# Loading the last query chunks of two batches late, on a kernel of linear attention followed by a two-layer ELU network

## The chip, the cores and the metric

The kernel runs on one core of one Trainium2 chip. The metric is the device time of one execution in microseconds, and lower is better. A change counts as faster or slower when it passes 2%. The span, from the first to the last traced instruction, is about 2 us shorter than the time.

## The reference, cut to what matters

```python
def _attn_ref(q, k, v):                      # q, k, v: 8 batches, 8 heads, 576 rows, 64 wide
    q_s = exp(q - max(q, -1));  q_s /= sum(q_s, -1)      # over the head's width
    k_s = exp(k - max(k, 2));   k_s /= sum(k_s, 2)       # over the sequence
    kv = einsum('bhsd,bhse->bhde', k_s, v)               # needs ALL of k and v of a batch
    return einsum('bhsd,bhde->bhse', q_s, kv)            # each row of q alone
def _moe_ref(x, w_in, w_out):                # x: 4608 x 512, w_in: 512 x 2048
    h = x @ w_in
    g = where(h > 0, h, exp(min(h, 0)) - 1)              # ELU
    return g @ w_out                                     # 4608 x 512
```

The asymmetry that the change uses is in the comments. A batch's kv needs every row of k and v. An output row needs only its own row of q.

## The kernel before

The program works in 9 blocks of 512 rows of x, but a batch has 576 rows, which are 9 chunks of 64. So block 0 takes chunks 0 to 7 of batch 0, and its ninth chunk is left for block 1. Of batch 1, block 1 takes 7 chunks and leaves 2. `split(b)` says where the cut is, and `ao_rest` makes the product for the leftover chunks. A *unit* is half a batch (4 heads), so q0 and q1 belong to batch 0, q2 and q3 to batch 1. `hg` is a group of hidden columns (256 of 2048) of one block, `kv` the k-v product, `W1` is w_in and `W2` w_out. A list scheduler orders the instructions of each engine from estimated durations; TensorE keeps its program order.

```python
    @staticmethod
    def split(b):
        if b < 2:
            return 8 - b
        ...

    def q_part(self, n, key):          # exp on ScalarE, sum and reciprocal on VectorE; all 9 chunks
        ...
    def q_mul(self, n, key, dmat):     # QS = exp(q) / sum, all 9 chunks
        ...
        S.add("dve", 1400, lambda e: e.tensor_tensor(qso, raw[:, :, :, :], rz, ALU.mult), ...)

    def tp(self, n, ps, key, evac="act"):      # transpose QS on TensorE, units 0 to 3 only
        ...
        def mm(e):
            for c in range(CH):                # CH = 9
                o = c * 128 if c < 5 else 1024 + (c - 5) * 128
                last = e.transpose(t16[:, o:o + 128], self.QS[al][:, c, :], self.ID[:, :])
            return last
        ...                                    # two evictions, of 5 and 4 chunks

    def exp_k(self, n, key):
        ek, flat = self.ek(n % 2), self.raw_flat(n % 2, "k")
        self.S.add("act", t_act(1152, False), lambda e: e.activation(...AF.Exp), ...)

    def program(self):
        ...
        for n, h in ((0, 0), (0, 1), (1, 0), (1, 1)):      # q of batch 0: unit 0 on SP, unit 1 on GpSimd
            src = self.src["q"][0, 4 * h + 2 * n:4 * h + 2 * n + 2, :, :].rearrange(
                "f (p c) d -> (f p) (c d)", c=CH)          # rows of 2304 bytes
            ...
        for n, t in ((0, "k"), (0, "v"), (1, "k"), (1, "v")):
            gp = self.load(n, t, "gp", -80, follow=gp)     # everything from here on: GpSimd's queue
        for s in range(4):
            gp = self.load_w1(s, -60, follow=gp)           # 4 parts of W1, 4 loads each
        ...
        self.hg_mm(0, 0, 3, (1,))
        self.hg_mm(0, 1, 2, (1,))
        self.ao_rest(0, 1, -60)                            # leftover of batch 0: in the startup
        for what in (0, "2q", 1, "3q", 2, "2k", "2v", "3k", "3v", 3, 4, 5):   # numbers: parts of W2
            ...
        for j in range(NBLK):
            for g in range(8):
                self.hg(j, g, order[g % 4], key, "gp" if j or g > 2 else "act" if g == 1 else "dve", ...)
            ...
            if j == 0:
                work = dict(zip((6, 9, 11, 19), (
                    lambda: self.tp(2, C, key), lambda: self.tp(3, Dd, key), lambda: kv([2, 3]),
                    first)))
            ...
            if j == 0:
                elem_q(2, k1)
                self.ao_rest(1, Dd, key)                   # leftover of batch 1: end of block 0
```

The softmax here doesn't subtract the row's maximum and nothing guards it: scores larger than these inputs give would overflow.

Of the kernel before, what the change touches and what calls it, by code (L numbers as in the profile page):

```python
# [18 lines left out]
CH = 9  # L19
# [16 lines left out]
class Sched:  # L36
# [49 lines left out]
    @staticmethod  # L86
    def parts(names):

        return [y for x in names for y in ([x + "h0", x + "h1"] if x in ("vR0", "vR1") else [x])]
# [168 lines left out]
class Gen:  # L258
# [13 lines left out]
    def alloc(self):  # L272
# [21 lines left out]
        self.RZK = [self.RZ[:, i, :] for i in range(2)]  # L294
        self.SEEN = a("SEEN", [16, 4, 16], F32)
# [35 lines left out]
    def load_half(self, n, t, h, key, follow):  # L331
# [6 lines left out]
                          tag=f"ld {t}{n}")  # L338

# [43 lines left out]
    def q_part(self, n, key):  # L383
# [3 lines left out]
        halves = (0, 1) if n < 2 else (slice(0, 2),)  # L387
        for h in halves:
            part = raw[:, h]
            part = part.rearrange("p c d -> p (c d)" if n < 2 else "p h c d -> p (h c d)")  # L390
            S.add("act", t_act(1152 // len(halves), False),
                  lambda e, part=part: e.activation(part, part, AF.Exp), key,  # L392
                  X=[self.q_res(n)[h]] if n < 2 else self.q_res(n), low=True, tag=f"expq{n}")
        for h in halves:
            z, src = zq[:, h], raw[:, h]
            if n > 1:
                z, src = z.rearrange("p h c -> p (h c)"), src.rearrange("p h c d -> p (h c) d")
            S.add("dve", 1350 if n > 1 else 750, lambda e, z=z, src=src: e.tensor_reduce(  # L398
                z, src, AX.X, ALU.add), key, R=self.q_res(n) if n > 1 else [f"qR{n}h{h}"],
                W=[f"ZQ{i}h0", f"ZQ{i}h1"] if n > 1 else [f"ZQ{i}h{h}"], low=True, tag=f"red{n}")  # L400
        S.add("dve", 270, lambda e: e.reciprocal(self.RZQ[i][:, :, :], self.ZQ[i][:, :, :]),
# [3 lines left out]
    def q_mul(self, n, key, dmat):  # L405
# [4 lines left out]
        rz = self.RZQ[i][:, :, :].unsqueeze(3).broadcast_to([128, 2, CH, D])  # L410
        qso = self.QS[al][:, :, :].rearrange("p c (h d) -> p h c d", h=2)
        S.add("dve", 1400, lambda e: e.tensor_tensor(qso, raw[:, :, :, :], rz, ALU.mult),  # L412
              key, R=qR + [f"RZQ{i}"], W=[f"QS{al}"], low=True, tag=f"mul{n}", port=True)
        if dmat:
# [3 lines left out]
                R=[f"QS{al}"], W=qR, dma=f"tp{i}{dmat}", nbytes=128 * 2304 * (4 if n < 4 else 1), low=True, tag=f"dtp{n}")  # L418
# [35 lines left out]
    def tp(self, n, ps, key, evac="act"):  # L454

        S = self.S
# [3 lines left out]

        def mm(e):
            for c in range(CH):
                o = c * 128 if c < 5 else 1024 + (c - 5) * 128
                last = e.transpose(t16[:, o:o + 128], self.QS[al][:, c, :], self.ID[:, :])
            return last
        S.add("pe", CH * 56 + 110, mm, key, R=[f"QS{al}", "ID"], X=bk, tag=f"tp{n}")
        for x, (c0, c1, o) in enumerate(((0, 5, 0), (5, 9, 1024))):
# [3 lines left out]
            if evac == "act" or x == 0:  # L471
                S.add("act", t_act(w, True), lambda e, dst=dst, src=src: e.activation(
                    dst, src, AF.Copy), key, W=[f"qsT{al}{x}"], X=[bk[x]], tag=f"evq{n}")
            else:
# [37 lines left out]
    def exp_k(self, n, key):  # L512
        ek, flat = self.ek(n % 2), self.raw_flat(n % 2, "k")
        self.S.add("act", t_act(1152, False), lambda e: e.activation(
            ek[:, :, :, :], flat.rearrange("p (h c d) -> p h c d", h=2, c=CH), AF.Exp),
            key, X=[f"kR{n % 2}"], low=True, tag=f"expk{n}")
# [90 lines left out]
    def ao_rest(self, b, ps, key, x=1):  # L607
# [4 lines left out]
        at = b * CH + c0  # L612
        for n in (2 * b, 2 * b + 1):
            i = n % 2

            def mm(e, i=i):
                for f in range(2):
                    last = e.matmul(P[:, f * 512 + i * w:f * 512 + i * w + w], self.MBLK[i][:, f, :],  # L618
                                    self.qsT[i][:, c0:c1, f * 64:f * 64 + 64], start=True, stop=True)
# [141 lines left out]
    def program(self):  # L761
# [6 lines left out]
        for n, h in ((0, 0), (0, 1), (1, 0), (1, 1)):  # L768
            src = self.src["q"][0, 4 * h + 2 * n:4 * h + 2 * n + 2, :, :].rearrange(
                "f (p c) d -> (f p) (c d)", c=CH)  # L770
            dst = self.RQ[n][:, h, :, :].rearrange("p c d -> p (c d)")
            eng = "gp" if n else "sp"
            op = S.add(eng, 450 if eng == "sp" else 760, lambda e, src=src, dst=dst: e.dma_start(dst, src),  # L773
                       -90, W=[f"qR{n}h{h}"], dma=f"q{n}h{h}", nbytes=128 * 2304,
# [8 lines left out]
        for n, t in ((0, "k"), (0, "v"), (1, "k"), (1, "v")):  # L783
            gp = self.load(n, t, "gp", -80, follow=gp)
# [177 lines left out]
```

## Time and profile before

| | before |
|---|---|
| time, median of 3 runs | 297.72 us (297.61 to 297.74) |
| time and span of the profiled run | 298.25 us, 296.4 us |
| TensorE busy | 98% of the span |
| idle time of its weight loads after 13.66 us | 0.49 us ahead of hidden group 4, 1.15 us ahead of batch 1's kv |

The last row comes from the timeline of the weight-load engine of the kernel before. Its columns are start, duration, engine, line, operation, operands and count, with the idle time ahead and its releaser in brackets. These are the lines of the two holes and the one ahead of the first:

```profile
16.41 5.33 PEld L654 LDWEIGHTS PS<-XT,W 128*128 128x128 f32 x24
22.24 7.15 PEld L654 LDWEIGHTS PS<-XT,W 128*128 128x128 f32 x32 [0.49 <-DVE GT L676]
...
42.59 0.67 PEld L491 LDWEIGHTS PS<-VB,KR 64*64 64x64 bf16 x72 [1.15 <-DVE VB L442]
```

I call these two places gates: TensorE reaches hidden group 4 of block 0 and may wait for W1's third part, and it reaches batch 1's kv and may wait for v. After the second gate it never waits again.

### The profile page before, as it was taken

To read this page: it belongs to the slowest core of one execution; us is meant where nothing else is said; L and a number is where in the kernel's file an instruction comes from. 1 tells how busy PE (TensorE), PEld (TensorE's weight loads), DVE (VectorE), ACT (ScalarE), POOL (GpSimd) and SP (SyncE) were. 2 spreads that over 40 slices of the span, in tenths; PEclk is the share of its full clock that TensorE was granted. 3 is DMA by queue.
4 is the path that set the end of the run, shared out by engine and by line. 5 is a ranking of instruction groups with operands and counts; after the bars stand their busy time and mean duration, and the time that the engine had idled before them with its cause. 6 is when DMAs were issued, how large, how long until landed. Compare 5 with 4: busy or idle time off the path is not lost.

```text
span 296.4 us, 4373 instructions
## 1 busy us (share of the span) xinstructions
PE 290.6 (98%) x1840; PEld 235.8 (80%) x1840; DVE 149.6 (50%) x167; ACT 152.3 (51%) x177; POOL 123.1 (42%) x133
## 2 busy tenths in 40 slices
PE   7999999999999999999999999999999999999995
PEld 2578878887888888878888888888878888888885
DVE  6857951978346913692268416760661046105600
ACT  5666366963666375546554565537541455125411
POOL 8998200762187035713372237313740055005500
PEclk9999999999999999999999999999999999999999
DMA  7999988927992598039901990099002210131022
GB/s 238 320 391 390 390 286 291 394 95 132 311 229 112 182 356 162 0 94 347 260 3 30 375 287 10 2 328 213 1 0 58 46 42 0 45 75 25 0 65 77
DMA packets 36675, 49.37 MB, mean 167 GB/s; under 512 B 16688, under 2 KB 17456, under 8 KB 36656
## 3 DMA queue, kind: packets, MB, share of 16 engines
q1 hardware_dynamic: 29872, 34.29, 40.5%
q0 software_dynamic: 6320, 14.29, 15.8%
q10 hardware_dynamic: 464, 0.53, 0.5%
q8 instruction: 14, 0.23, 0.3%
q14 instruction: 5, 0.04, 0.0%
HBM read 36.70 MB, written 9.44 MB: 156 GB/s over the span
## 4 chain that ended last, share of the span: by engine, by line
PE 85%; DMA 7%; POOL 6%; issue 0%; DVE 0%; ACT 0%; POOLq 0%
PE PS L700 41%; PE PS L654 39%; DMA VR<-in_v_dram 7%; POOL W L347 3%; PE PS L491 2%; PE PS L584 2%; PE PS L618 1%; POOL W L358 1%; POOL KR L315 1%; POOL VR L315 0%; POOL QR L315 0%; POOL QR L773 0%; DVE VB L442 0%; ACT OSB L733 0%; POOL ID L749 0%
## 5 line engine op out<-in xcount | busy, mean ns | idle before, releaser
L683 DVE SCALAR_TENSOR_TENSOR GT<-ESB,PS 128x1024 fp32r<-128x1024 f32 x69 | 84.0, 1221 | 116.6 <-POOL ESB L680 116.5
L700 PE MATMUL PS<-W,GT 128*128 128x512 f32 (+1 forms) x592 | 136.4, 386 | 0.0
L654 PE MATMUL PS<-XT,W 128*128 128x512 f32 x576 | 133.0, 390 | 0.1
L654 PEld LDWEIGHTS PS<-XT,W 128*128 128x128 f32 x576 | 107.8, 188 | 22.9 <-DVE GT L676 0.5
L700 PEld LDWEIGHTS PS<-W,GT 128*128 128x128 f32 x592 | 108.0, 188 | 21.6
L680 POOL TENSOR_SCALAR ESB<-ESB 128x1024 f32<-128x1024 f32 x69 | 73.7, 1075 | 100.1 <-ACT ESB L668 100.1
L668 ACT ACTIVATE ESB<-PS 128x1024 f32<-128x1024 f32 x72 | 73.8, 1028 | 51.5 <-PE PS L654 51.5
L714 ACT ACTIVATE OSB<-PS 128x512 f32<-128x512 f32 x35 | 20.7, 598 | 55.5 <-PE PS L700 55.1
L438 POOL CAST VB<-VR 128x1152 bf16<-128x1152 f32 x12 | 14.5, 1212 | 46.6 <-DMA VR<-in_v_dram 46.6
L398 DVE TENSOR_REDUCE ZQ<-QR 128x18 f32<-128x1152 f32 (+1 forms) x18 | 21.7, 1212 | 2.6 <-ACT QR L392 2.6
L412 DVE TENSOR_TENSOR QS<-QR,RZQ 128x1152 f16<-128x1152 f32 x16 | 21.5, 1353 | 0.4
L392 ACT ACTIVATE QR<-QR 128x1152 f32<-128x1152 f32 (+1 forms) x18 | 18.6, 1054 | 4.1 <-DMA QR<-in_q_dram 4.0
L425 POOL CAST qsT<-QR 128x1152 fp32r<-128x1152 f16 x12 | 13.8, 1152 | 10.0 <-DMA QR<-QS 10.0
L432 ACT ACTIVATE KR<-KR 128x1152 bf16<-128x1152 f32 x14 | 15.9, 1169 | 3.8 <-DMA KR<-in_k_dram 3.8
L604 ACT ACTIVATE XT<-PS 128x640 fp32r<-128x640 f32 (+1 forms) x12 | 8.2, 738 | 15.4 <-PE PS L584 15.4
L347 POOL DMA_DIRECT2D W<-in_moe_w_in_dram x16 | 10.0, 1357 | 0.0
L640 PE MATMUL PS<-IDLE 128*128 128x512 f32 (+1 forms) x14 | 8.5, 732 | 1.5 <-DVE IDLE L752 1.5
L358 POOL DMA_DIRECT2D W<-in_moe_w_out_dram x6 | 9.1, 2416 | 0.0
L628 ACT ACTIVATE XT<-PS 128x1024 fp32r<-128x1024 f32 (+3 forms) x8 | 6.8, 846 | 1.1 <-PE PS L618 1.1
L491 PEld LDWEIGHTS PS<-VB,KR 64*64 64x64 bf16 x504 | 4.7, 107 | 3.3 <-DVE GT L683 1.8
L584 PE MATMUL PS<-qsT,MBLK 128*128 128x320 f32 (+3 forms) x32 | 7.1, 338 | 0.0
L640 PEld LDWEIGHTS PS<-IDLE 128*128 128x128 f32 (+1 forms) x14 | 2.6, 210 | 5.6 <-issue 2.3
(46 smaller groups left out, 83.8 us busy)
## 6 DMA issues: line engine op xcount, KB each, us to landing
out_dram<-OSB SPq DMA_DIRECT2D x67, 128.0 KB, 3.6
QR<-in_q_dram SPq DMA_DIRECT2D x12, 576.0 KB, 8.6
KR<-in_k_dram SPq DMA_DIRECT2D x12, 576.0 KB, 6.1
VR<-in_v_dram SPq DMA_DIRECT2D x12, 576.0 KB, 6.8
W<-in_moe_w_in_dram POOLq DMA_DIRECT2D x16, 256.0 KB, 9.6
W<-in_moe_w_out_dram POOLq DMA_DIRECT2D x3, 1024.0 KB, 16.3
KR<-in_k_dram POOLq DMA_DIRECT2D x4, 576.0 KB, 13.6
VR<-in_v_dram POOLq DMA_DIRECT2D x4, 288.0 KB, 14.6
```

The lines of the kernel that those rows point to most:

```text
L347: "gp", 530, lambda e, kc=kc: e.dma_start(self.W1[:, kc, sl], w[kc, :, :, sl]), key,
L392: lambda e, part=part: e.activation(part, part, AF.Exp), key,
L398: S.add("dve", 1350 if n > 1 else 750, lambda e, z=z, src=src: e.tensor_reduce(z, src, AX.X, ALU.add), key, R=self.q_res(n) if n > 1 else ...
L412: S.add("dve", 1400, lambda e: e.tensor_tensor(qso, raw[:, :, :, :], rz, ALU.mult), key, R=qR + [f"RZQ{i}"], W=[f"QS{al}"], low=True, tag= ...
L432: S.add("act", t_act(1152, False), lambda e: e.activation(ek[:, :, :, :], flat.rearrange("p (h c d) -> p h c d", h=2, c=CH), AF.Exp), key, ...
L438: self.cv[n] = S.add("gp", 1250, lambda e: e.tensor_copy(VB[:, :, :, 0:D], raw[:, :, :, :]), key, R=rv, W=[f"VB{i}0", f"VB{i}1"], low=True ...
L654: last = e.matmul(P[:, t * 512:(t + 1) * 512], self.W1[:, kc, tt * 128:(tt + 1) * 128], self.XT[:, kc, rc:rc + BLK], start=(kc == 0), stop ...
L668: S.add("act", t_act(1024, True), lambda e: e.activation(esb[:, :], P[:, :], AF.Exp), key, W=[f"E{i}"], X=self.banks(ps), tag=f"exp{j}.{g}")
L680: S.add("gp", 1120, lambda e: e.tensor_scalar(esb[:, :], esb[:, :], 1.0, 0.0, ALU.min, ALU.max), key, X=[f"E{i}"], tag=f"min{j}.{g}", port ...
L683: S.add("dve", t_dve(1024), lambda e: e.scalar_tensor_tensor(gt, esb[:, :], -1.0, P[:, :], ALU.add, ALU.max), key, R=[f"E{i}"], W=gw, X=se ...
L700: last = e.matmul(dst, GT[:, jj, ts * 128:(ts + 1) * 128], self.W2[:, jj, cols], start=(jj == 0), stop=(jj == 15))
L714: S.add("act", t_act(512, True), lambda e: e.activation(osb[:, :], src, AF.Copy), key, W=[f"O{i}0", f"O{i}1"], X=[f"b{bk}"], tag=f"evo{jb} ...
```

## The change

The intent is to keep out of the load queue, in the first 42 us, what is not needed there. The ninth chunk of batch 0's q goes from in front of k to the middle of W1's first part, and chunks 7 and 8 of batch 1's q go behind W2. The two leftover products move to where a later block needs them. W2's loads stay as they are. The diff, cut to its core (helpers for resource names, evictions and hints to the scheduler are left out):

```diff
@@ q_part, q_mul: for units 0 and 1 only the first 8 chunks @@
+        w = self.split(0) if n < 2 else CH
@@ new @@
+    def load_q1(self, n, part, eng, key, after=(), follow=None):   # "m": 7 chunks, "r": 2 chunks
+        cs = slice(0, self.split(1)) if part == "m" else slice(self.split(1), CH)
+        ...
+    def q_piece(self, n, part, key):       # exp, sum, reciprocal, multiply of one part
+        ...
+        if part == "r":                    # and, for 2 chunks: transpose by DMA on SP, cast on GpSimd
+            ...
+    def load_last(self, key, follow):      # ninth chunk of both units: 512 rows of 256 bytes
+        src = self.src["q"][0, :, :, :].rearrange(
+            "(h u f) (p c) d -> c (f p) (h u) d", h=2, u=2, c=CH)[CH - 1]
+        ...
+    def q_last(self, key):                 # its exp, sum, reciprocal, two multiplies
+        ...
@@ tp @@
-            for c in range(CH):
+            for c in range(count):         # count = 8; chunk 7 of batch 0 holds the ninth chunk's rows
@@ exp_k: two halves for k1 @@
+        for h in (slice(0, 2),) if n == 0 else (slice(0, 1), slice(1, 2)):
@@ program @@
-                "f (p c) d -> (f p) (c d)", c=CH)
+                "f (p c) d -> (f p) (c d)", c=CH)[:, 0:w * D]          # rows of 2048 bytes
...
+            if (n, t) == (1, "k"):
+                for h in range(2):
+                    gp = self.load_half(n, t, h, -80, gp)
+                continue
...
-            gp = self.load_w1(s, -60, follow=gp)
+            gp = self.load_w1(s, -60, follow=gp, kcs=(0, 1))
+            if s == 0:
+                gp = self.load_last(-60, gp)
+            gp = self.load_w1(s, -60, follow=gp, kcs=(2, 3))
...
-        self.ao_rest(0, 1, -60)
+        self.q_last(-60)
...
+            elif what[1] == "q":
+                gp = self.load_q1(int(what[0]), "m", "gp", -50, follow=gp)
...
-                self.hg(j, g, order[g % 4], key, "gp" if j or g > 2 else "act" if g == 1 else "dve",
+                self.hg(j, g, order[g % 4], key, "gp" if j or g > 3 else "act" if g % 2 else "dve",
...
+                if j == 0:
+                    for n in (2, 3):
+                        self.ldq = self.load_q1(n, "r", "sp", key, after=self.w2, follow=self.ldq)
...
-                    work = dict(zip((6, 9, 11, 19), (
-                        lambda: self.tp(2, C, key), lambda: self.tp(3, Dd, key), lambda: kv([2, 3]),
-                        first)))
+                    def both():
+                        self.ao_rest(0, Dd, key)
+                        kv([2, 3])
+                    work = dict(zip((6, 8, 11, 19), (
+                        lambda: self.tp(2, C, key), lambda: self.tp(3, Dd, key), both, first)))
+                elif j == 1:
+                    def both():
+                        self.ao_rest(1, Dd, key)
+                        ...
+                        convert(2, key)
+                        ...
+                        kv([n0, n1])
+                    work = {5: both, 12: aos}
...
-                self.ao_rest(1, Dd, key)
```

## The prediction

> **What bounds the kernel now.** I read the page first: one core, span 296.4 us, granted clock full in every slice. Then the chain of waits, which tells where the end is set.
>
> ```profile
> PE 290.6 (98%) x1840; PEld 235.8 (80%) x1840; DVE 149.6 (50%) x167; ACT 152.3 (51%) x177; POOL 123.1 (42%) x133
> ...
> DMA  7999988927992598039901990099002210131022
> ```
>
> ```profile
> 5.80 9.89 POOL W L347 x16
> ...
> 20.37 0.45 POOL VR L315
> 20.82 21.23 DMA VR<-in_v_dram
> 42.05 0.02 issue
> 42.07 0.48 DVE VB L442
> 42.55 0.04 issue
> 42.59 0.77 PE PS L491 x68
> 43.37 2.06 PE PS L700 x8
> ...
> 48.46 14.59 PE PS L654 x64
> ```
>
> The columns of the second fence are start, duration, what. From 42.59 us to the end at 293.45 the chain is TensorE alone, one piece after the other without a gap: 250.9 us of pure matrix work. Before 42.59 it isn't TensorE but a queue of transfers: GpSimd issues them all by 22 us, and the last unit of v for batch 1 lands at 42.05. The DMA digits of the page are 8 or 9 through most of this stretch. So a change can gain in two ways only: let batch 1's kv product (L491) start before 42.59, or take matrix work out of what follows it.
>
> Next, how TensorE spends the time up to 42.59: the windows view, cut where TensorE's idle times are (columns: length of the window, busy time of each engine with counts, clock, DMA share, GB/s), and the waits of the first 50 us.
>
> ```profile
> 13.66:21.80 8.14, 8.14 (x40) 6.75 (x38) 4.26 (x6) 4.56 (x7) 8.14 (x15) 1.00 1.28 394
> 21.80:22.24 0.44, 0.37 (x2) 0.00 (x1) 0.14 (x1) 0.44 (x2) 0.44 (x5) 1.00 1.28 377
> 22.24:41.44 19.20, 19.17 (x97) 15.71 (x98) 14.42 (x15) 10.48 (x12) 7.92 (x10) 1.00 1.23 390
> 41.44:42.59 1.15, 0.42 (x2) 0.00 (x0) 0.79 (x2) 1.15 (x3) 0.00 (x0) 1.00 1.10 299
> ```
>
> ```profile
> PEld PS L491 <- DVE VB L442: 1.2, 1, 1.2
> ...
> PEld PS L654 <- DVE GT L676: 0.5, 1, 0.5
> ```
>
> Two holes in the weight loads. At 41.44 they stop for 1.15 us until v is converted. The same place one block later has an idle time of 0.35 us that is put down to issue, so about 0.80 us is a real wait. At about 21.8 they stop for 0.5 us, before hidden group 4 of block 0. The view blames VectorE, but the elu that frees group 4's bank (group 0's) ended at 20.66 in the timeline. Group 4 also needs the third part of W1, and the trace's landing record of the twelfth W1 load ends at 22.4; such records end some 0.2 us after their reader starts (k of unit 0: record 8.72, its exp starts at 8.51). So that hole is W1's, and the DMA stream paces TensorE at both. Where nothing waits, 64 matmuls take 14.51 us (227 ns each).
>
> In the startup the same stream gates: exp of k1 waits for k1 until 11.48, v1 lands at about 12.85 and its kv product starts at 13.02, the first W1 load lands at about 13.55 and the first hidden matmul starts at 13.66.
>
> **What the Trainium skill says.** "DMA: Bandwidth & Descriptors", section "Issuing engines are not separate DMA queues": loads from any engine share the same 16 DMA engines. The trace agrees: the stream moves 390 GB/s whatever is in it, so bytes taken out of GpSimd's queue and loaded later count as time only while that queue is the gate. The same page, "Specifications", puts the size for line rate at 512 B or more, and "Why small descriptors are slow (HBM only)" gives 11 cycles in place of 8 for 256 B. No load in this trace has such rows, so I take it as an estimate for the new 256 B rows. "Anatomy of one DMA — SWDGE (gpsimd) path" puts most of a fixed 2 us into the receipt of the last byte. Here the bytes nearly stop at 42.6 (35 GB/s from 43 to 44), while the last W2 landing is recorded at 44.85, so a landing can come 2 us after its bytes.
>
> **The change, part by part.**
>
> (a) Batch 0's q loads lose the ninth chunk: 4 x 32 KB = 128 KB less in front of k0. At 390 GB/s that is 0.33 us, which all of k0, v0, k1, v1 and the first two W1 loads should land earlier. k1 in two halves lets ACT's exp after the last landing be about 0.68 in place of 1.16 us. But v1 (12.85) and W1 (13.55) gate next, so only 0.33 us of it counts: first hidden matmul at about 13.3.
>
> (b) The ninth chunks come back as one load of 128 KB in 512 rows of 256 B, after two of W1's sixteen loads. At the full rate 0.33 us, with twice the cost for short rows 0.67 us; I take 0.33 to 0.65. So every later load of GpSimd's queue is 0 to 0.3 us later than before, until (d). GpSimd's own issue (two more, 0.7 to 1 us each) is hidden: the first W1 load is issued at 5.7 and lands at 13.6.
>
> (c) The leftover product of batch 0 (L618, four matmuls, 0.53 us of TensorE at 16.08) leaves the startup and goes just ahead of batch 1's kv. The hidden groups 0 to 3 then run 0.3 + 0.5 us sooner, and TensorE reaches group 4 at about 21.0 in place of 21.8. There it meets W1's twelfth load, which now lands at 22.2 to 22.5 in place of 22.2. The whole startup gain becomes a longer wait at group 4 (about 1.3 in place of 0.45 us).
>
> (d) q2 and q3 lose 2 of 9 chunks: 2 x 128 KB, 0.66 us less in front of v3. With (a) and (b), v3 lands 0.33 - (0.33 to 0.65) + 0.66, so 0.35 to 0.65 us earlier, at 41.4 to 41.7. The conversion takes 0.46 us and the hop 0.05, so v lets kv start at 41.9 to 42.25.
>
> (e) TensorE's arrival at kv: before, 22.24 + 19.55 = 41.79 (42.59 less the 0.80 of real wait). After: 22.2 to 22.5, plus 19.55, plus 0.55 for batch 0's leftover, less 0.11 for one transpose fewer in each of the two groups of nine (0.51 us for nine weight loads): 42.2 to 42.5. This is later than v's 41.9 to 42.25, so TensorE and no longer v sets the start: about 42.3, a gain of 0.3 us.
>
> (f) After kv: batch 1's leftover product (0.40 us at 48.06) moves from the end of block 0 into block 1, and costs the same there. Its two chunks, now a separate small piece for each unit, add per unit an exp of 256 (about 0.42 us on ACT), reduction, reciprocal and multiply (about 1.0 us on DVE), a small DMA transpose and a cast of 0.4 us on GpSimd. VectorE is idle for 5.56 us before 52.58, and the leftover is wanted only at about 69, so this is beside TensorE's work. The casts of q4 and q5 (2.25 us from 72.35, their data landing only then) are followed by their product at 75.42; moving their place in the program behind the leftover (about 69) takes nothing from that.
>
> (g) ELU of groups 2 and 3 by VectorE and ACT, not GpSimd: it keeps a GpSimd busy with issuing (until about 25) out of group 3's chain, whose bank is needed at 27.7 and was freed at about 27.3. Protection, no gain by itself.
>
> Sum: (e) -0.3 us, the rest 0: 297.72 - 0.3 = 297.4 us.
>
> **The rivals.**
>
> First rival: v stays the gate. If the short rows cost nothing, W1 lands on time and TensorE arrives at 42.2, v at 41.9; if TensorE also waits less at group 4, the start falls to the v gate and the gain is up to 0.65 us (297.1). One thing could bring that: a 16 KB instruction fetch at 18.25 takes 1.16 us on one DMA engine, and from there the spread between the first and last of the sixteen completions of a load grows from 1.05 to 2.3 us, which delays W1's third part and all later landings. The change removes 12 matrix instructions before that point, so it may come later in the W1 stream. I reckon some 0.7 us later, still before the twelfth W1 load.
>
> Second rival: the leftover of batch 0 waits for the eviction of the transposed q3, which in the kernel before ran from 41.62 to 42.79, behind exp of k3. If ACT's order stays so, the leftover starts near 42.4 and kv near 42.9: 0.3 us slower (298.0). Against it: the transposes of q3 come two plan steps nearer to those of q2 than before, and one eviction of 1024 replaces two, so ACT should do it before k3 lands at about 40.
>
> Third rival: the added pieces of (f) upset an in-order queue (SP's transposes, GpSimd's mins) in block 1 and leave a hole in TensorE's 14.5 us runs. There is room on every engine, so I give it a tenth, and 0.3 to 1 us.
>
> **Range and chances.** The gate times leave 0 to 0.6 us of gain; the two losses pull the other way by 0.3 to 0.5, and runs scatter by 0.1: 296.8 to 298.1. Two per cent would be 6 us. The whole of TensorE's waiting after 13.66 is 1.3 us, so faster by 2% is excluded by the sum, and slower by 2% would need a stall of a kind that I don't see.
>
> **What would show it.** In the changed profile: first hidden matmul at about 13.3; no L618 piece near 16; a hole of about 1 us in the weight loads before group 4, ending at 22.2 to 22.5; the kv product at about 42.3 right behind batch 0's leftover, with little or no wait on v's conversion; then an unbroken chain of TensorE of 250.8 us. Wrong would be: group 4 starting before 22, a wait on ACT's eviction ahead of the leftover, or new holes between 48 and 80.

## The result, and the profile after

| | time, median | range | runs | span, median |
|---|---|---|---|---|
| before, same chip | 297.73 us | 297.61 to 297.79 | 4 | |
| after | 298.05 us | 297.60 to 298.45 | 4 | 295.95 us |

The ratio is 1.0011, with a 95% interval of 0.9994 to 1.0028: the same. The prediction was 297.4 us, "same", 296.8 to 298.1. The range held, but the small gain that I expected is not there.

The profiled run of after was its fastest, 297.60 us. First the counts and the DMA digits from its page:

```profile
PE 289.2 (98%) x1836; PEld 235.8 (80%) x1836; DVE 151.3 (51%) x177; ACT 153.1 (52%) x180; POOL 123.3 (42%) x136
...
DMA  7999988978991696039902990098002110230022
...
q8 instruction: 14, 0.23, 0.3%
```

Four matmuls less, and ten more instructions on VectorE. The DMA digits are the same 8 or 9 up to 59 us; the one that moved most is the ninth (59 to 66 us), 7 in place of 2, where loads behind W2 now fall, and no gate lies there. The third line, the same in both pages, will matter later: 14 packets of 16 KB are instruction fetches, and they travel on the same DMA engines as the loads. The chain of waits of after:

```profile
16.39 12.97 PE PS L740 x56
29.37 6.35 PE PS L786 x28
...
38.54 2.81 PE PS L786 x12
41.35 0.37 PE PS L704 x4
41.72 0.74 PE PS L573 x67
42.45 2.05 PE PS L786 x8
...
47.17 14.51 PE PS L740 x64
```

The chain of before was a queue of transfers up to 42.05. Here it is TensorE from 16.39 on: hidden groups (L740) without a hole at group 4, out products (L786), then batch 0's leftover (L704, four matmuls) and kv (L573) right behind it. The weight-load timeline of after says the same; beside the lines of before, the hole at 22.24 is gone and kv starts at 41.67 in place of 42.59:

```profile
16.36 12.58 PEld L740 LDWEIGHTS PS<-XT,W 128*128 128x128 f32 x56 [0.61 <-DVE XT L684]
...
38.33 2.59 PEld L786 LDWEIGHTS PS<-W,GT 128*128 128x128 f32 x12
40.96 0.65 PEld L704 LDWEIGHTS PS<-qsT,MBLK 128*128 128x128 f32 x4
41.67 0.67 PEld L573 LDWEIGHTS PS<-VB,KR 64*64 64x64 bf16 x72
```

And the windows of after, cut as before (length, busy time with counts of TensorE, its weight loads, VectorE, ScalarE and GpSimd, clock, DMA share, GB/s):

```profile
13.60:21.80 8.20, 7.96 (x34) 6.29 (x35) 5.33 (x10) 4.48 (x6) 8.20 (x16) 1.00 1.31 384
21.80:40.92 19.12, 19.12 (x97) 15.61 (x96) 13.96 (x16) 12.34 (x13) 8.06 (x11) 1.00 1.23 388
40.92:41.67 0.75, 0.75 (x6) 0.60 (x4) 0.47 (x1) 0.00 (x0) 0.00 (x0) 1.00 1.23 371
```

TensorE is busy for the whole of the last two rows: the leftover's 0.75 us stands where before had 1.15 us of waiting. The chain follows whichever ended last, and here that hides a tie. The last load of v landed at 41.13 (before: 42.05), and its conversion ended at 41.63:

```profile
41.16 0.47 DVE L518 CAST VB<-VR 128x576 bf16<-128x576 f32 x1 [0.29 <-DMA VR<-in_v_dram]
```

The leftover's last weight load ended at 41.60. So kv starts 0.54 us after v's landing, just as in before (42.05 to 42.59): v is still a gate, and TensorE arrives with it.

This trace is 0.92 us better at kv than the trace of before. Its span is 0.98 us shorter (295.47 against 296.45), but its time only 0.65 us (297.60 against 298.25), and the medians say +0.3. Two questions follow. Does the trace of after show the typical run? And where do 0.3 us go between span and time?

### The profile page after: what moved, and what is told of

It reads as the page before. It is cut to its first block, busy times and chain, and to the rows that moved or that the text cites. A ratio compares the mean times of both kernels' runs of the same rounds, so it can differ in the third digit from the quotient of the medians.

```text
span 295.5 us, 4387 instructions
## 1 busy us (share of the span) xinstructions
PE 289.2 (98%) x1836; PEld 235.8 (80%) x1836; DVE 151.3 (51%) x177; ACT 153.1 (52%) x180; POOL 123.3 (42%) x136
## 3 DMA queue, kind: packets, MB, share of 16 engines
q1 hardware_dynamic: 30992, 34.61, 41.4%
## 4 chain that ended last, share of the span: by engine, by line
PE 96%; DMA 2%; POOL 1%; issue 0%; ACT 0%; POOLq 0%
PE PS L786 45%; PE PS L740 44%; DMA VR<-in_v_dram 2%; PE PS L668 2%; PE PS L573 2%; PE PS L704 1%; PE PS L544 1%; PE PS L634 0%; POOL QR L860 0%; POOL KR L325 0%; PE PS L726 0%; ACT OSB L819 0%; PE PS L616 0%; POOLq L1061 0%
## 5 line engine op out<-in xcount | busy, mean ns | idle before, releaser
L769 DVE SCALAR_TENSOR_TENSOR GT<-ESB,PS 128x1024 fp32r<-128x1024 f32 x68 | 82.8, 1220 | 110.6 <-POOL ESB L766 110.6
L786 PE MATMUL PS<-W,GT 128*128 128x512 f32 (+1 forms) x592 | 136.5, 386 | 0.0
L740 PE MATMUL PS<-XT,W 128*128 128x512 f32 x576 | 132.6, 389 | 0.4 <-issue 0.2
L740 PEld LDWEIGHTS PS<-XT,W 128*128 128x128 f32 x576 | 108.0, 188 | 23.3 <-DVE XT L684 0.6
L786 PEld LDWEIGHTS PS<-W,GT 128*128 128x128 f32 x592 | 108.0, 188 | 21.6
L766 POOL TENSOR_SCALAR ESB<-ESB 128x1024 f32<-128x1024 f32 x68 | 71.3, 1049 | 100.7 <-ACT ESB L754 100.6
L421 DVE TENSOR_REDUCE ZQ<-QR 128x18 f32<-128x1152 f32 (+1 forms) x16 | 18.8, 1180 | 2.4 <-ACT QR L415 2.3
L436 DVE TENSOR_TENSOR QS<-QR,RZQ 128x1152 f16<-128x1152 f32 (+1 forms) x14 | 18.5, 1334 | 0.3
L415 ACT ACTIVATE QR<-QR 128x1152 f32<-128x1152 f32 (+1 forms) x16 | 16.0, 1025 | 1.3 <-DMA QR<-in_q_dram 1.1
L726 PE MATMUL PS<-IDLE 128*128 128x512 f32 (+1 forms) x14 | 7.5, 647 | 1.5 <-DVE IDLE L838 1.5
L668 PEld LDWEIGHTS PS<-qsT,MBLK 128*128 128x128 f32 x32 | 5.5, 189 | 1.1 <-DVE MBLK L645 0.4
```

Of the source, the lines that this page charges most:

```text
L415: lambda e, part=part: e.activation(part, part, AF.Exp), key,
L421: S.add("dve", 1350 if n > 1 else 680, lambda e, z=z, src=src: e.tensor_reduce(z, src, AX.X, ALU.add), key, R=self.q_res(n) if n > 1 else ...
L436: S.add("dve", 1260 if n < 2 else 1400, lambda e: e.tensor_tensor(qso, raw[:, :, 0:w, :], rz, ALU.mult), key, R=qR + [f"RZQ{i}"], W=[f"QS{ ...
L668: return e.matmul(P[:, f * 512:f * 512 + n_], M[:, f, :], T[:, c0:c1, f * 64:f * 64 + 64], start=True, stop=True)
L740: last = e.matmul(P[:, t * 512:(t + 1) * 512], self.W1[:, kc, tt * 128:(tt + 1) * 128], self.XT[:, kc, rc:rc + BLK], start=(kc == 0), stop ...
L766: S.add("gp", 1120, lambda e: e.tensor_scalar(esb[:, :], esb[:, :], 1.0, 0.0, ALU.min, ALU.max), key, X=[f"E{i}"], tag=f"min{j}.{g}", port ...
```

## The experiments

Each run is compared with the kernel before, run on the same chip in the same rounds. From here on I read the same columns from every trace. The table is put together from the weight-load timelines, the trace's records of DMA packets (the first instruction fetch inside the kernel) and of landings (the last load of v), and the run's time; all in us.

| trace | first hidden matmul | group 4 starts (hole) | first fetch | last v lands | kv starts | span | span − kv | time − span |
|---|---|---|---|---|---|---|---|---|
| before | 13.66 | 22.24 (0.49) | 18.01 | 42.05 | 42.59 | 296.45 | 253.86 | 1.80 |
| e2, before again | 13.72 | none | 17.44 | 41.73 | 42.27 | 296.14 | 253.87 | 1.79 |
| e5 | 13.65 | 22.14 (0.40) | 18.21 | 41.94 | 42.48 | 296.32 | 253.84 | 1.80 |
| e11 | 13.37 | 21.70 (0.23) | 17.07 | 41.49 | 42.03 | 295.72 | 253.69 | 1.83 |
| e10 | 13.30 | 21.59 (0.20) | 17.56 | 40.81 | 41.35 | 295.03 | 253.68 | 1.81 |
| e13 | 13.99 | none | 17.37 | 41.06 | 41.60 | 295.26 | 253.66 | 1.81 |
| after | 13.60 | none | 20.63 | 41.13 | 41.67 | 295.47 | 253.80 | 2.13 |
| e1, after again | 13.40 | 22.96 (1.47) | 20.40 | 42.19 | 42.83 | 296.59 | 253.76 | 2.13 |
| e3 | 13.43 | none | 20.40 | 41.34 | 41.88 | 295.72 | 253.84 | 2.14 |
| e4 | 13.67 | 22.38 (0.94) | 19.47 | 41.54 | 42.20 | 295.96 | 253.76 | 2.14 |
| e8 | 13.52 | none | 24.77 | 41.75 | 42.29 | 296.09 | 253.80 | 2.16 |
| e9 | 13.11 | none | 20.18 | 42.21 | 42.75 | 296.65 | 253.90 | 2.20 |
| e7 | 13.54 | 22.36 (0.72) | 16.63 | 41.59 | 42.21 | 297.72 | 255.51 | 2.14 |
| e12 | 14.22 | none | 21.08 | 41.12 | 42.35 | 298.05 | 255.70 | 2.13 |

Fetches and landings are counted here from the zero of the timelines. The prediction, the expectations and their figures (18.25 and 20.87 for the fetch; 8.72, 22.4 and 44.85 for landings) have them 0.24 us too late.

Three columns carry most of what follows. **Last v lands**: kv starts 0.54 us after it in ten of the fourteen traces, 0.62 to 0.66 us in e1, e4 and e7, and 1.23 us in e12 alone. So v gates kv in ten traces, and in three TensorE comes later by 0.1 us. **Span − kv** is 253.66 to 253.90 in all but two traces, so what happens after kv hardly depends on the kernel, and a median span tells the typical kv start. For before, 296.1 (its median span on chip 10) less 253.85 is 42.25; for after, 295.95 less 253.8 is 42.15. **Time − span** has two values, 1.8 and 2.1 to 2.2, and nothing between; the runs without a trace, whose spans are known to 0.1 us, fall into the same two groups.

### e1 and e2: both kernels unchanged, once more

No edit. My theory was that the first pair of traces misleads because kv's start scatters.

> The changed kernel unchanged, to see its scatter and a second trace. Its first trace (span 295.5 us, the fastest of its four runs) shows the kv product of batch 1 at 41.68 us, 0.9 us earlier than in the trace of before, with no hole at hidden group 4 and the 16 KB instruction fetch at 20.87 instead of 18.25 us; yet the medians say 0.3 us slower. Theory 1 (the stream and the fetch): the scatter comes from the first 45 us; a slower run shows the fetch early (near 18 to 19.5) and a hole at group 4 of about 0.5 to 1 us, kv at 42.2 to 42.6. Rival (the rest of the kernel): kv again at 41.7, and a slower run has its time after 48 us. Median expected 297.6 to 298.4, ratio 0.999 to 1.003.

> The kernel before, unchanged: the null. Ratio 1.000 within 0.001. Theory 1: its trace shows a fetch near 18 and a hole of about 0.5 us at group 4 again, kv at 42.2 to 42.6; if the first trace was an unlucky one (its run took 298.25, its other runs 297.6 to 297.8), kv is about 0.5 us earlier, at 42.1.

Measured: after again 298.05 us (297.70 to 299.41, 6 runs, span 295.95), ratio 0.9992 (0.9961 to 1.0023); before again 297.82 us (span 296.0), 0.9987 (0.9954 to 1.0020); before in the same rounds 297.96 us (span 296.1). A few runs of before (3 of 11), of e2 (1 of 6) and of e4 below (2 of 6) took 299.8 to 300.1; none of them was traced. The record gives them a granted clock of 0.993 or 0.994, where all other runs of these rounds have 0.998 or more. 0.6 to 0.7% of TensorE's 290 us would be 1.7 to 2.0 us, an estimate from these figures that matches their excess of 1.8 to 2.1. Without the slow-clock runs, the ratio of the means is 1.0011 for after again and 0.9995 for before again. The weight-load timeline of after again, and the piece of its chain of waits that ends at group 4:

```profile
16.20 5.29 PEld L740 LDWEIGHTS PS<-XT,W 128*128 128x128 f32 x24 [0.65 <-DVE XT L684]
22.96 7.17 PEld L740 LDWEIGHTS PS<-XT,W 128*128 128x128 f32 x32 [1.47 <-DMA W<-in_moe_w_in_dram]
...
42.83 0.67 PEld L573 LDWEIGHTS PS<-VB,KR 64*64 64x64 bf16 x72
```

```profile
12.56 10.36 DMA W<-in_moe_w_in_dram
```

The same program as in the trace above: there no hole at group 4 and kv at 41.67, here a hole of 1.47 us, which the view puts down to W1's load, and kv at 42.83. So one trace of after stands for nothing alone, and the typical kv start of 42.15 lies between the two. Two forecasts missed: the fetch was not earlier in this slower run (20.40 against 20.63), and the trace of before again has no hole at group 4.

What makes the difference can be read from the landing records. A load completes in sixteen parts. In thirteen of the fourteen traces, from the first instruction fetch on, the spread between the first and the last of these parts is larger by 0.7 to 1.5 us, and stays about so to the end of the stream. In after again it grows from 1.1 to 2.6 us exactly at W1's twelfth load (recorded landing 22.92); in the first trace of after only from 1.37 to 1.73 us, behind that load (21.54). At v's last load the first part comes at nearly the same time in both (39.50 and 39.41), but the last at 42.19 and 41.13. The first fetch itself, one packet, takes 1.10 to 1.16 us. Why it costs the stream more in one run than in another stays open. The Trainium skill, "Runtime: NRT & Kernel Launch", section "Instruction fetch mechanics", says that instructions are fetched in blocks of 16 KiB (256 instructions) and that crossing a boundary is "mostly hidden". The traces agree with the size: each fetch is a packet of 16 KB. But that sentence is about the engine that fetches; here the fetch isn't hidden from the loads beside it. The change moves it from 17.1 to 18.2 us in the four traces of before and its variants to about 20.5, into the arrival of W1's third part.

### e3: the short-row load behind W1

```diff
-            if s == 0:
-                gp = self.load_last(-60, gp)
             gp = self.load_w1(s, -60, follow=gp, kcs=(2, 3))
+        gp = self.load_last(-60, gp)
```

If the load of the ninth chunks delays W1, moving it behind W1 should remove the wait at group 4.

> The load of batch 0's last chunk (512 rows of 256 B) moves from between W1's second and third load to behind all of W1. In the changed kernel W1's third load lands 0.8 us later, counted from v1, than before. Theory 1: the first hidden matmuls with kc 2 and 3 start about 0.4 us earlier (15.95 in place of 16.36), W1's third part lands 0.5 to 0.8 earlier, but v3 and W2 land as before, so kv is at 41.7 or at the v gate (41.4): time 0 to 0.3 us less than the changed kernel, and less scatter. Rival (place does not matter): same time as the changed kernel within 0.1 us.

Measured: 298.15 us (span 296.0), ratio 0.9991 (0.9960 to 1.0022), in the same rounds as e1: no different from after. TensorE meets no hole at group 4, but at the next gate it waits for v:

```profile
41.88 0.67 PEld L573 LDWEIGHTS PS<-VB,KR 64*64 64x64 bf16 x72 [0.68 <-DVE VB L518]
```

The load's place doesn't matter: v comes later in the same queue whichever side of W1 the bytes lie on. What the load costs can be read too, as the distance between the recorded landings of W1's first and third load: 1.91 to 2.05 us with it between them in five traces, 1.35 to 1.43 without it in nine. So 128 KB in rows of 256 bytes took 0.5 to 0.7 us of the stream, where the 390 GB/s of the other loads would give 0.33.

### e4: batch 0's q loaded whole again

```diff
-                "f (p c) d -> (f p) (c d)", c=CH)[:, 0:w * D]
+                "f (p c) d -> (f p) (c d)", c=CH)
...
-            if s == 0:
-                gp = self.load_last(-60, gp)
```

The first four loads have 2304-byte rows again, there is no short-row load, and the ninth chunks are computed from the rows already there (by one ScalarE instruction more; this is left out of the cut). The late leftover product and all else stay.

> Batch 0's q is loaded whole again in the first four loads, and the late load of 256 B rows is gone; its last chunk is still computed late, from the raw tile (one ACT instruction more). Theory 1: v1 lands 0.25 later, W1's third load and all after it 0.3 to 0.6 us earlier than in the changed kernel (0.8 us of short rows gone, 0.3 put in front), so W1's third part and v3 come earlier: kv at 41.2 to 41.5, time 0.2 to 0.5 us less than the changed kernel. Rival (startup counts most): the first hidden matmul 0.3 us later shifts everything, time 0.3 us more than the changed kernel.

Measured: 297.85 us, ratio 0.9999 (0.9959 to 1.0038); four runs at 297.49 to 298.10 and two at 300.0 and 300.1. Median span 295.75, 0.2 less than after again in the same rounds. The trace still has a hole of 0.94 us at group 4 without any short-row load in the queue. So that load is not the cause of the hole, and kv at 42.20 misses the forecast of 41.2 to 41.5. But this is the slowest of the four runs at full clock. These four have a median of 297.59 us and a span of 295.5, both some 0.45 less than after again, which is within the 0.2 to 0.5 forecast, though from four runs against six. Time − span stays at 2.14, so the load isn't what sits outside the span either.

### e5: before with more semaphores

The 0.3 us between span and time needed theories of its own. After has more load tags, and each tag is a semaphore; resetting more of them might cost time outside the span.

```diff
-                          dma=f"{t}{i}{eng}", nbytes=128 * 4608,
+                          dma=f"{t}{n}{eng}", nbytes=128 * 4608,
```

> The kernel before with the same instructions in the same order, but every q, k and v load of the later batches has a semaphore of its own (about 28 more). In all runs so far that have both numbers, the time exceeds the traced span by 1.80 and 1.83 us for the kernel before and by 2.08 to 2.16 for the changed one and its variants, whose traces name 70 landing semaphores instead of 63. Theory S (each DMA semaphore costs time outside the span, 0.28 us for 7, 40 ns each): the difference grows to about 2.9 us and the median to about 299.0, while the span stays at 296. Rival (the extra 0.28 us has another source, more instructions or another start): difference stays 1.8, median 297.9.

Measured: 297.85 us, ratio 0.9998 (0.9986 to 1.0010). The trace shows 94 landing semaphores in place of 63, and time − span is 1.80. The theory fell.

### e7 and e8: moving the instruction fetch

In e7, 12 one-column matmuls are added near the start (24 instructions on TensorE), which should bring the fetch forward. In e8 six idle matmuls of the startup are not emitted, which should put it behind W1.

```diff
e7:
         self.spin(3, 0, long=True)
+        S.add("pe", 300, lambda e: [e.matmul(self.bank(0)[:, 0:1], ...one column...) for _ in range(12)][-1],
+              -5, R=["IDLE"], X=["b0"], tag="tiny")
e8:
+            if o.tag == "spin16":
+                continue
```

> The changed kernel with 12 one-column matmuls (24 TensorE instructions) put among the warming ones, about 0.3 us in time in which TensorE waits anyway. Theory 1 (the 16 KB instruction fetch comes after a number of TensorE instructions, and its 1.1 us on one DMA engine delays every later landing): the fetch comes 24 instructions, so about 2.5 us, earlier, near 18 us as before, W1's third part always lands 1.1 us late at 21.9 to 22.6, a hole of 0.6 to 1.3 us at hidden group 4, kv at 42.0 to 42.6; median within 298.0 to 298.6 with no fast runs at 297.7. Rival (fetch time has nothing to do with the count, or the lag comes from something else): as the changed kernel.

> The changed kernel without its six short warming matmuls (12 TensorE instructions less), all else in the same order. Theory 1: the fetch comes about 1.3 us later, near 22, behind W1's third part: no hole at hidden group 4, kv at 41.6 to 41.8 in every run, median 297.6 to 297.8, less scatter. Rival (TensorE then runs slower in the startup because it is not kept warm): first hidden matmul later than 13.6 and slower matmuls, median 298 or more.

Measured: the fetch moved as meant, to 16.63 us in e7 and to 24.77 us in e8, and the growth of the spread moved with it, to W1's seventh load in e7 and to W2's first in e8. The time did not follow: e7 298.33 us (297.70 to 299.86), ratio 1.0018 (1.0000 to 1.0036); e8 298.25 us, 1.0005 (0.9993 to 1.0017). First the weight-load timeline of e7, then that of e8:

```profile
22.36 7.15 PEld L740 LDWEIGHTS PS<-XT,W 128*128 128x128 f32 x32 [0.72 <-DMA W<-in_moe_w_in_dram]
```

```profile
16.30 12.58 PEld L742 LDWEIGHTS PS<-XT,W 128*128 128x128 f32 x56 [0.63 <-DVE XT L686]
...
42.29 0.67 PEld L575 LDWEIGHTS PS<-VB,KR 64*64 64x64 bf16 x72 [0.74 <-DVE VB L520]
```

With the fetch ahead of W1's third part there is a hole of 0.72 us at group 4. With it behind W1 there is none, and the same lag appears at kv as a wait of 0.74 us for v. The fetch decides at which gate TensorE pays, not how much it pays by kv: 42.21 and 42.29. I had expected a gain from e8, and there was none. Its rival, a TensorE slower in the startup, didn't show either: the first hidden matmul is at 13.52 us. Time − span is 2.14 and 2.16, so it isn't the length of TensorE's program that sets it.

The profiled run of e7 also shows the third rival of the prediction at work. The next two fences are the GpSimd casts of q4 and q5 in block 1, in the timeline of after and in that of e7:

```profile
69.69 1.15 POOL L501 CAST qsT<-QR 128x1152 fp32r<-128x1152 f16 x1 [5.82 <-DMA QR<-QS]
72.40 1.15 POOL L501 CAST qsT<-QR 128x1152 fp32r<-128x1152 f16 x1 [1.56 <-DMA QR<-QS]
```

```profile
73.75 3.37 POOL L501 CAST qsT<-QR 128x1152 fp32r<-128x1152 f16 x2 [8.52 <-DMA QR<-QS]
```

In after, the casts start at 69.69 and 72.40, and the last ends 0.9 us ahead of the product that needs it (before: 0.8). In e7 the first cast waits for its data until 73.75 and the second ends at 77.12, 3.6 us later than in after, so TensorE stops for 1.8 us in the middle of block 1. That is the whole excess of its span − kv. The margin is thin in these kernels. The untraced runs at about 300 us are another matter, as far as the record shows: their granted clock is 0.993 or 0.994, that of the traced stalls in e7 and e12 0.999 and 1.0. (The 299.41 us of after again is at full clock.)

### e9: batch 1's two late chunks back in front of v

```diff
             elif what[1] == "q":
                 gp = self.load_q1(int(what[0]), "m", "gp", -50, follow=gp)
+                gp = self.load_q1(int(what[0]), "r", "gp", -50, follow=gp)
...
-                        self.ldq = self.load_q1(n, "r", "sp", key, after=self.w2, follow=self.ldq)
```

> Undoes part (d): the two last chunks of q2 and q3 (2 x 128 KB, in rows of 512 B) go back to GpSimd's queue ahead of v3 and W2's last parts; all else as in the changed kernel. By the prediction v3 lands 0.66 us later (about 42.0 in place of 41.37 or 42.4 with the lag), and kv starts at 42.5 to 43.1: 0.5 to 0.8 us slower than the changed kernel where v is the gate, 0.2 to 0.4 where W1's third part is. Rival (v3 is not the gate in most runs of the changed kernel): same time within 0.15 us.

Measured: 299.30 us, ratio 1.0043 (1.0030 to 1.0056), 1.2 us above after and more than expected. Two things in its weight-load timeline:

```profile
29.48 6.24 PEld L786 LDWEIGHTS PS<-W,GT 128*128 128x128 f32 x28 [0.92 <-DVE GT L769]
...
42.75 0.67 PEld L573 LDWEIGHTS PS<-VB,KR 64*64 64x64 bf16 x72 [0.72 <-DVE VB L518]
```

The wait for v at kv, 0.72 us at a later time, is the expected part: each of the two loads took about 0.42 us of the stream. The hole of 0.92 us at 29.48 was not expected. There VectorE's ELU waits for GpSimd's half of it, and GpSimd is still issuing loads, two more than in after. So the size of e9 mixes bytes with issue time, and I take only its direction from it: bytes ahead of v cost.

### e10: batch 1's part of the change alone

This starts from before and takes only the split of q2 and q3 and the move of batch 1's leftover.

```diff
 before, plus load_q1 and q_piece as in the change, and
-            for c in range(CH):
+            for c in range(count):             # 9 for units 0 and 1, 7 for units 2 and 3
...
-                    work = dict(zip((6, 9, 11, 19), (
+                    work = dict(zip((6, 8, 11, 19), (
...
+                elif j == 1:                   # batch 1's leftover and convert(2) ahead of kv
...
-                self.ao_rest(1, Dd, key)
```

> The kernel before with part (d) alone: q2 and q3 load seven chunks ahead of v3 and the last two behind W2 on SP, batch 1's leftover product moves into block 1; batch 0's startup, its leftover near 16 us, the first k1 load and the ELU choices stay as before. By the prediction's sum: group 4 starts at about 22.2 as before, TensorE would arrive at kv at 41.55 (41.79 less 0.22 for two transposes fewer in each group), v lands at 41.1 to 41.4 and lets kv start at 41.6 to 41.9: 0.5 to 0.7 us earlier than the kernel before (42.27 and 42.59 in its traces), span 295.4 to 295.7. Rival (parts (a) to (c) are what shortened the span): kv at 42.2 or later, span as before, 296.1. The time less the span tells whether the extra 0.3 us comes with this part (2.1) or with batch 0's part (1.8): median 297.4 if 1.8, 297.7 if 2.1.

Measured: 297.08 us (296.83 to 297.53, 6 runs), ratio 0.9977 (0.9965 to 0.9989); before in the same rounds 297.76 us. The median span fell from 295.9 to 295.25. The interval excludes 1: this is a real, small gain of 0.7 us, though "same" by the rule of 2%. Its chain of waits, the counterpart of the one in the prediction:

```profile
20.52 20.29 DMA VR<-in_v_dram
40.81 0.02 issue
40.83 0.48 DVE VB L489
...
41.35 0.77 PE PS L541 x66
```

The shape of before is kept (v's transfers, its conversion, kv), and the transfer ends at 40.81 in place of 42.05 (41.73 in the trace of before again). Time − span is 1.81, that of before.

### e11: before with padding instructions

To see whether the 0.3 us hangs on more instructions, before gets 12 tiny instructions on VectorE, 3 on ScalarE, 5 on GpSimd and 4 tiny loads on SP.

```diff
+        for i in range(12):
+            S.add("dve", 60, lambda e: e.memset(self.PAD[:, 0:1], 0.0), -94, W=["PAD0"], tag="pad")
+        ...                                    # likewise 3 on act, 5 on gp, 4 touch loads on sp
```

> The kernel before with 12 tiny instructions more on VectorE, 3 on ACT, 5 on GpSimd and 4 one-KB loads more on SP, all in idle time near the start: more instructions on these engines than the changed kernel has. Theory (the extra 0.3 us outside the span comes with the length of the programs): time less span 2.1. Rival (it comes from something else, such as the last part of a queue or the place of tiles): 1.8. The span stays within 0.4 us of the kernel before.

Measured: 297.85 us, ratio 1.0001 (0.9988 to 1.0014), time − span 1.83. Longer programs on VectorE, GpSimd and SP don't make it. One reading is left over: in all traces with 2.1 us or more ScalarE has 224 or 225 recorded instructions (its issues included), in all with 1.8 it has 223 or fewer. A threshold there would fit; I had no run that tests it.

### e12: batch 0's q and k1 whole

e4 with k1 in one load again; its exp stays in two halves.

```diff
 e4, and
-            if (n, t) == (1, "k"):
-                for h in range(2):
-                    gp = self.load_half(n, t, h, -80, gp)
-                continue
```

> The changed kernel with batch 0's q loaded whole at the start, no late short-row load (as in the run with q0 whole), and k1 in one load: GpSimd issues 35 loads, as many as in the kernel before, while batch 0's leftover product still stands in front of batch 1's kv. Theory G (time outside the span grows when GpSimd issues more than 35 loads: 35 gave 1.80 to 1.84 us, 36 to 39 gave 2.11 to 2.21): difference 1.8. Rival (it belongs to another part of batch 0's change, such as the leftover's place): 2.1. Span: if the leftover's new place is what costs (theory of the prediction's step (c): TensorE waits at group 4 for W1's third part and then does 0.55 us more before kv), 295.4 to 296.0, that is 0.3 to 0.7 us more than with part (d) alone (295.0 to 295.7). Median 297.2 to 297.8.

Measured: 300.85 us (300.18 to 302.51), ratio 1.0108 (1.0081 to 1.0134). It was meant to test whether the number of GpSimd's loads (35, as in before) sets the 0.3 us; it doesn't, time − span is 2.13. The 3 us are of another kind, as the waits of its weight loads show:

```profile
PEld PS L670 <- POOL qsT L503: 2.1, 1, 2.1
...
PEld PS L618 <- ACT KR L600: 1.3, 1, 1.3
```

The first is the stall in block 1 again. The second is a wait for k1's exp in the startup: the scheduler put two evictions between its two halves, and the second half starts at 12.66. Two of the six runs (302.12 and 302.51) had the granted clock of 0.994 as well. So this run is confounded and says nothing on the worth of k1's halves.

### e13: e10 with k1 in two halves

```diff
 e10, and
+            if (n, t) == (1, "k"):
+                for h in range(2):
+                    gp = self.load_half(n, t, h, -80, gp)
+                continue
```

> Part (d) alone, the best kernel so far (297.08 us, span 295.0 to 295.7), with k1 in two loads and two exps: GpSimd issues 36 loads. Theory G: time less span 2.1, median 297.3 to 297.4 at an unchanged span. Rival: 1.8 and a median of 297.1. The startup gain of the halves: the prediction says none, as v1 and W1 gate the first hidden matmul; if it is worth something the span falls below 295.0.

Measured: 297.29 us (296.77 to 297.48), ratio 0.9976 (0.9958 to 0.9994), time − span 1.81. The same ratio as e10: the halves add nothing and cost nothing. At kv TensorE and v arrive together; the wait is about the usual hop of 0.35 us:

```profile
41.60 0.67 PEld L541 LDWEIGHTS PS<-VB,KR 64*64 64x64 bf16 x72 [0.39 <-DVE VB L489]
```

## Why the prediction was right or wrong

**The class and the bound were right.** TensorE is a chain without gaps behind kv, and the change touches at most what lies before. Span − kv is the same within 0.24 us in twelve of fourteen traces.

**The start from one trace was wrong.** Its base was late by 0.34 us. The sum began at kv 42.59, the trace of a run of 298.25 us, and was taken off 297.72, the median of others. The typical kv before is 42.25. From there to the predicted 42.3 is no gain. The typical kv after, 42.15, was predicted to 0.15 us, so the gain in the span is about 0.1 to 0.15 us, not the 0.3 of step (e). That the time still fell into the range is partly luck: its upper end of 298.1 was meant for losses in the chain of waits, and what filled it was the late base and a loss outside the span that the sum didn't have. The slower profiled run was listed among the times that I had.

**(a) Four shorter q loads, first hidden matmul at 13.3.** Measured 13.40 to 13.60 in five traces with the shorter rows and 13.11 in e9; before has 13.37 to 13.72 in its four (e2, e5 and e11 with it). The 0.33 us are inside the scatter of the startup. The remark that k1's halves count for nothing held (e13).

**(b) The short-row load, 0.33 to 0.65 us.** Measured 0.5 to 0.7, the upper end of the range. The Trainium skill, "DMA: Bandwidth & Descriptors", "Why small descriptors are slow (HBM only)", gives 11 cycles for 8 at 256 bytes, from which an estimate is 0.33 × 11/8 = 0.46 us, a little less than measured. The load returns all of what (a) took out, and 0.2 to 0.4 us more, to every later load of the queue. That its place doesn't matter is shown by e3.

**(c) A wait of about 1.3 us at group 4.** This is the two-valued step. Traces of after and its variants show either none or 0.7 to 1.5 us. The mechanism of the prediction (TensorE early, W1's twelfth load late) is what e1 shows. Where there is no hole, the lag comes at kv as a wait for v of about 0.7 us (e3, e8) or is filled by the leftover product (after).

**(d) 0.66 us less in front of v3.** e10 is this step alone, and it gained 0.7 us in time and 0.65 us in span. This is the one part of the change that pays.

**(e) TensorE and no longer v sets kv.** This is the step that failed. kv still starts 0.54 us after v's last landing, as in before, in after itself (41.13 to 41.67) and in e3, e8 and e9; in e1, e4 and e7 TensorE is later by 0.08 to 0.12 us only. The leftover's term was 0.55 us. The trace of after has 0.75 us between the stop of the other weight loads and kv, where the usual hop is 0.35: 0.40 us net, which fill a wait for v rather than add to the time.

**(f) and (g), beside TensorE's work.** They held in the traces of after and in e10. What I had rated a tenth, a stall in block 1, happened in the profiled runs of e7 and e12, 1.8 and 2.1 us. The margin of 0.8 to 0.9 us there was in the trace of before, but I only looked at whether the change took from it.

**Two readings of the first trace.** That a landing record ends some 0.2 us after its reader starts is the zero that was 0.24 us off: k of unit 0 landed at 8.48, ahead of its exp at 8.51, and W1's twelfth load at 22.18, ahead of group 4 at 22.24. This makes the case for W1 at that hole stronger. And the last bytes before the W2 landing (44.61 on the timelines' zero) were not those of 42.6: the queue's last packet ends at 44.19, 0.42 us ahead of it, at the end of a trickle of 15 packets after 43. So this trace doesn't show a receipt of 2 us.

**The step that is missing.** The sum moved the time by what it moved the span. In all eight runs traced with batch 0's part of the change, 0.33 us more lie outside the span (2.13 to 2.20 against 1.79 to 1.83). It isn't the number of semaphores (e5), TensorE's program length (e7, e8), the program length of VectorE, GpSimd or SP (e11), the number of GpSimd's loads (e12), k1's halves (e13), the short-row load (e4) or batch 1's part (e10). Left are, among others, ScalarE's program length, the new tiles and the choice of engine for ELU. The cause is open. (A draft that reused semaphores in after was found to have races and so could not be run; the record has nothing of it.)

**The account.** Batch 1's part gives 0.7 us. Batch 0's part takes back about 0.6 us in the span (typical kv 42.15 against 295.25 − 253.7 = 41.55 in e10) and 0.33 us outside it. 0.7 − 0.6 − 0.33 is a loss of 0.2 us, and the measured medians differ by 0.3 us. The traces place a part of the 0.6. The first of the sixteen parts of v's last load comes at 39.16 and 39.18 in e10 and e13, at 39.14 and 39.17 in e4 and e12, where batch 0's q is whole, and at 39.32 to 39.71 in after, e1, e3, e7 and e8: 0.15 to 0.55 us that come with the shorter rows and the short-row load. The leftover product ahead of kv cost 0.12 us at most, but for e12. The rest is not placed: how far the last part comes behind the first at this load (1.6 to 2.7 us) differs more from trace to trace than the kernels do.

**The rivals.** The first (v stays the gate) is what after, e3, e8 and e9 show, without the gain of 0.65 us that I gave it: v landed at 41.1 to 42.2 in these traces, and the typical kv of 42.15 less 0.54 puts it at 41.6, inside the 41.4 to 41.7 of step (d); it was the base that was late. The second (the leftover waits for the eviction of q3) did not happen in after; e12 has 0.6 us of it. The third is the stall of e7 and e12.

**The better version.** e10 beats before by 0.23%, and against its own rounds of before it stands better than after did (0.9977 against 1.0011 and 0.9992; e10 and after were not run in the same rounds). It is batch 1's part without batch 0's, and e13 (0.9976) repeats the gain on another chip.

## What to carry to other kernels

Moving bytes back in a queue pays only when they pass a gate that really waits, and when no work moves in the other direction: batch 1's chunks passed v and gained their 0.7 us, batch 0's passed k and came back ahead of both gates, in shorter rows. Where two chains meet, read when each arrives: the chain of waits of after named TensorE alone, and v had come at the same time. For differences under a per cent, compare the profiled run with the median before taking its times as the base of a sum, and trace the same kernel twice, since the place of a wait can change from run to run. Read time minus span as well: a change can cost something that no trace of the engines shows.

## What the Trainium skill lacked or had wrong

- "Runtime: NRT & Kernel Launch", "Instruction fetch mechanics", doesn't say what a fetch does to loads under way. Beside the load stream the first fetch of 16 KB took 1.10 to 1.16 us, and the spread of the sixteen completions of each later load was larger by 0.7 to 1.5 us in thirteen of fourteen traces (before: from 1.05 to 2.3 us).
- No page has what makes time minus span 1.8 us in one kernel and 2.1 in another of nearly the same program. The number of landing semaphores doesn't (94 against 63: 1.80 us both).
